# A transformer block in one kernel: new keys, engines and margins for the list schedule of its end

## The chip, the core and the metric

The kernel runs on one core of one Trainium2 chip. Its time is the device time of one execution in microseconds (us), start to end. The engines are named as in the profile: PE is the matrix engine (PEld its weight loads), DVE the vector engine, ACT the scalar engine, POOL is GpSimd, and SP is the engine that only issues DMAs here. Each of them works through its own queue of instructions in order, and waits at an instruction until the semaphores that it needs have been raised.

## The reference

One block of a transformer on 2048 rows of 512 values, all in float32: a LayerNorm with scale and shift from a condition vector, sliding-window attention (32 heads of 16, window 256), the output projection with a gate, a second LayerNorm, and a gated feed-forward network (FFN) with 1792 inner columns.

```python
    def _A_ref(x, wqkv, wo):
        ...
        scores = jnp.einsum("bhqd,bhkd->bhqk", q, k) * (Dh ** -0.5)
        ...
        mask = (idx[:, None] - idx[None, :] >= 0) & (idx[:, None] - idx[None, :] < W)
        scores = jnp.where(mask[None, None], scores, -1e9)
        p = _softmax(scores, axis=-1)
        o = jnp.einsum("bhqk,bhkd->bhqd", p, v)
        return (lambda x, *d: x.transpose(*d))(o, 0, 2, 1, 3).reshape(B, S, D) @ wo
    def _B_ref(x, w1, w3, w2):
        ...
        h = _silu(gate) * up
        out = jnp.einsum("bsf,fd->bsd", h, w2)
        return out
    ...
    h = _layernorm(x, axis=-1) * (1 + ca) + sa
    x = x + ga * _A_ref(h, A_wqkv, A_wo)
    h = _layernorm(x, axis=-1) * (1 + cb) + sb
    x = x + gb * _B_ref(h, B_w1, B_w3, B_w2)
```

## The kernel before

**Products.** Every precise product is made of three matmuls: an operand is split into a rounded high part (a copy on ACT) and the low rest (a subtraction on DVE or POOL), and high x high, high x low and low x high are summed in PSUM. So each new operand costs one ACT copy and one subtraction before PE can use it.

**Attention.** The rows are four blocks b of 512, the heads eight groups g of four. One unit is a pair (g, b); 32 units run in order u = 4g + b. A unit has a part a (products for queries and keys, L438), a part b (the row maxima: scores L485, maximum on DVE L494) and a part c (scores L753, masks by DVE L761 and L773 or by POOL L780 and L795, exponentials on ACT L768, values L721). At the end of a unit ACT copies its output (L815) and SP stores it to o_dr in DRAM (L818). The order of all that is written out by hand as offsets in time (the dictionary X).

**The end.** From the time TS = 229.9 in these offsets on, the remaining attention instructions are not simply emitted. They are put into a list with fixed times, which the function us() works out (KEY and the slopes TW), and everything else, the fillers, is given to a list scheduler, class Sched. A filler has an engine, an estimated duration, tiles that it reads and writes, and a key. The method deal() keeps the ready fillers of each engine in the order of their keys and takes, engine by engine, the first one that can start when the engine is free, or else the one that can start soonest; fixed operations go in when their time comes. A filler on PE that needs a result of ACT, DVE or POOL counts that result as ready PEM microseconds after its estimated end. A DMA (o.kb not zero) is given a time on one modelled wire (RATE KB per us), is kept out of the way of urgent row transfers of attention (QUIET), and its landing is the time at which its users become ready. The order that comes out is the order in which the instructions stand in the engines' queues; the chip knows nothing of the modelled times.

**The fillers.** The dictionary K holds most of their keys and some engines. In order of their work:

- load_x1 brings the residual rows x1 back (keys x1, xb, xl; tiles of the first half and of the second, x1a and x1b). load_wo loads and splits the output weights (key wo).
- o_sums (L1068 load, L1072 reciprocal on DVE, L1073 store) turns the softmax sums into factors (keys os and ol). o_part scales a quarter k of the outputs of block b: two loads (L1087, L1092), a product (L1104), a copy on ACT (L1096) and a subtraction (L1099). Keys pl (k = 3) and pe (the others); K["by"][b][k] names the engine of the product and that of the subtraction.
- o_proj multiplies block b by the output weights (L1116, 48 matmuls, key o[b] with steps of 0.27 for rows and 0.06 for quarters); add_stats adds the result to x1 on DVE and collects the sum for LayerNorm (L985, L990), and ACT squares it (L993).
- ln2 does the second LayerNorm of blocks 0 and 1 (key l2): the root on POOL (L1007), scaled rows on ACT (L1236), transposes on PE (L1250, keys l2 + 4 and l2 + 9), the modulation on ACT (L1254), sums and differences of the operands (L1267) and their splits (L1273, L1275).
- ffn does a step p of seven for one half of the rows. Each step has two sets (n = 0, 1) of seven up products, Strassen's scheme for two by two blocks (L1378), with sums on DVE and POOL (L1401 to L1421), a split (L1449, L1452), and the down products into x1 (L1471, L1476). Steps are fl apart, the first at f behind the modelled end of attention. load_w loads and splits the weights of a step (L1174, split L967 and L968, keys w0 and w), load_w2 those of the down product, and de puts off some of the last down products.
- Blocks 2 and 3 make the second half of the FFN. half_rows (key hr) and half_sums make their LayerNorm and operands during the first half and store them to DRAM, and load_b (key l3) loads the seven pairs of operands (L1353) and splits them at the start of the second half. K["be"] names the engines of the 14 subtractions (L968 into the tiles b).

PSUM has seven banks for all fillers, named st, mx and pj, beside the attention's po.

Of the kernel before, what the change touches and what calls it, by code (L numbers as in the profile page):

```python
# [112 lines left out]
class Sched:  # L113
# [36 lines left out]
    def deal(self):  # L150
# [5 lines left out]
        banks, fixed = list(self.banks), list(self.fixed)  # L156
        held = dict.fromkeys(CAPS, 0)
        given = dict.fromkeys(CAPS, 0)
        order, self.dealt = [], []

        def push(o):
            insort(ready[o.eng], (o.key, o.seq, o))

# [4 lines left out]
        while left:  # L168
            best = None
            for e, lst in ready.items():  # L170
                t, pick = free[e], None
                for key, seq, o in lst:
                    s = o.est
                    new = [b for b in o.bank if b.i is None]
                    if new:
# [6 lines left out]
                        s = max(s, at)  # L182
                    if o.kb:

                        b = max(s, t)
                        end = max(wire, b + 1.5) + o.kb / RATE + o.more - QUIET
                        s = max([s] + [u + 0.01 for u in self.urgent if b <= u < end])
# [24 lines left out]
            s, o = best  # L212
# [11 lines left out]
            if o.kb:  # L224
                s = max(s, lanes.pop(0))
# [17 lines left out]
                    banks[b.i] = b.end  # L243
                    held[b.use] -= 1
            for u in o.users:
                m = PEM if u.eng == "PE" and o.eng in ("ACT", "DVE", "POOL") else 0.0
                u.est = max(u.est, s + (o.lat + m if u.eng != o.eng or o.kb else o.occ))
                u.need -= 1
                if not u.need:
                    push(u)  # L250
# [5 lines left out]
INF = float("inf")  # L256
RATE = 320.0

QUIET = 1.5
KEY = 1.715  # L260
TS = 229.9

# [1 line left out]
def us(t):  # L264

    return KEY * (min(t, TW[0]) - TS + TW[2] * max(0.0, min(t, TW[1]) - TW[0]) + TW[3] * max(0.0, t - TW[1]))


TW = (231.0, 241.0, 0.8, 0.65)

KINDS = dict(product=("PE", 0.235), mix=("POOL", 1.25), qk_rows=("SP", 0.65), out=("ACT", 0.5), job=("POOL", 2.0),
             job_dma=("SP", 0.5), scores=("PE", 0.19), top=("DVE", 0.5), parts=("DVE", 0.4), turn=("PE", 0.11), cut=("ACT", 0.16),
# [1 line left out]
             far=("PE", 0.125), part=("POOL", 0.92), side=("ACT", 0.53), far_side=("ACT", 0.27), side_mask=("POOL", 0.92),  # L274
             side_probs=("ACT", 0.53), values=("PE", 0.66), cut_all=("ACT", 0.48), store=("SP", 0.45))
NPE = 3

PEM = 0.8

BY = ((("POOL", "POOL"),) * 3 + (("DVE", "DVE"),), (("POOL", "POOL"),) * 3 + (("DVE", "DVE"),),  # L280
      (("POOL", "DVE"),) * 3 + (("DVE", "DVE"),), (("POOL", "POOL"),) * 4)
K = dict(be=(('DVE', 'DVE'), ('DVE', 'POOL'), ('DVE', 'POOL'), ('POOL', 'POOL'), ('POOL', 'DVE'),
         ('POOL', 'DVE'), ('DVE', 'DVE')), hr=0.109, de=7.098, wo=-0.159, x1=5.764, xb=-29.382,
         xl=0.241, os=-0.129, ol=(-15.316, -4.484, -6.572, 4.956), pl=(3.999, 1.87, -4.828,
         102.62), pe=(0.982, -5.962, 56.258, 232.622), o=(1.381, 8.497, 20.124, -0.531), n=(1, 1,
         2, 1), w0=62.113, l2=0.424, f=1.543, fl=40.897, by=((('POOL', 'POOL'), ('DVE', 'DVE'),
         ('DVE', 'POOL'), ('DVE', 'DVE')), (('DVE', 'DVE'), ('DVE', 'POOL'), ('DVE', 'DVE'),
         ('DVE', 'POOL')), (('POOL', 'POOL'), ('POOL', 'DVE'), ('DVE', 'POOL'), ('POOL', 'DVE')),
         (('POOL', 'DVE'), ('DVE', 'POOL'), ('DVE', 'POOL'), ('DVE', 'POOL'))), w=0.559, dn=1.412,
         ds=0.003, l3=-0.027)  # L290
@with_exitstack
def block_kernel(ctx: ExitStack, tc: tile.TileContext, x, wqk, wv, wo, w13, w2, c, wmod, out):
    nc = tc.nc
# [653 lines left out]
    def dma(fn, key, reads, writes, kb=256, hold=False, occ=0.45, more=0.0):  # L947
        o = sch.op("SP", fn, occ, key, reads, writes, lat=2.0)
        o.kb, o.more = kb, more
        if hold:  # L950
            o.est = max(0.0, key)
# [7 lines left out]
    def on_eng(e):  # L959
        return nc.vector if e == "DVE" else nc.gpsimd  # L960

    def split(hi, lo, key, kh, kl, n=512, eng="POOL"):

        def src():
            return lo().bitcast(F32)
        kh, kl = (y if isinstance(y, list) else [y] for y in (kh, kl))
        sch.op("ACT", lambda: nc.scalar.activation(hi(), src(), AF.Copy), act(n), key, kl, kh)  # L967
        sch.op(eng, lambda: on_eng(eng).tensor_tensor(  # L968
            out=lo(), in0=src(), in1=hi().bitcast(F32), op=ALU.subtract),
               0.06 + 0.0024 * n if eng == "POOL" else 0.85, key, kl + kh, kl)  # L970
# [71 lines left out]
    def o_of(b):  # L1042
        return "p" if b == 1 else "o"
# [34 lines left out]
    def o_part(b, k, key):  # L1078
# [23 lines left out]
        dma(spread, key, [("r_dr", b, 2 * k), ("r_dr", b, 2 * k + 1)], [rn], 256, occ=0.67, more=0.1)  # L1102
        by, minus = K["by"][b][k]
        sch.op(by, lambda: on_eng(by).tensor_tensor(out=v["ot"], in0=v["ot"], in1=v["rt"], op=ALU.mult),  # L1104
# [4 lines left out]
    def o_proj(b, key):  # L1109
        for i in range(4):  # L1110
            bk = Bank("dn")
            t = 4 * b + i
            for k in range(KC):
                def go(i=i, k=k, bk=bk):
                    for n, (h, w) in enumerate(PARTS):
# [3 lines left out]
                sch.op("PE", go, 3 * MM[512], key + 0.27 * i + 0.06 * k,  # L1119
                       [y for kk in (range(K["n"][b]) if k == 0 else (k,)) for y in  # L1120
                        ((o_of(b), 0, kk), (o_of(b), 1, kk), ("wo", 0, kk), ("wo", 1, kk))], [bk])
# [222 lines left out]
    def load_b(key):  # L1344

        for n, m in enumerate((B11, T2, T3, T1, B21, T4, B22)):
            for k in range(2):
# [3 lines left out]
                else:  # L1351
# [3 lines left out]
                split(lambda m=m, k=k: BB[m, k][0], lambda m=m, k=k: BB[m, k][1], key + 0.1 * n,  # L1355
                      ("b", m, k, 0), ("b", m, k, 1), eng=K["be"][n][k])

    downs = []

    def ffn(half, p, key, fl):  # L1360
# [96 lines left out]
        def down():  # L1457
            load_w2(p, last, key + fl * (K["dn"] + K["ds"] * 8))
            for t in range(2):
                for i in range(4):  # L1460
                    at = 8 * half + 4 * t + i
                    bk = Bank("dn")
                    kk = key + fl * (1 + K["dn"] + K["ds"] * (4 * t + i)) + (
                        K["de"] if half and p == NP - 2 else 0.0)

# [140 lines left out]
```

## Time and profile before

| | |
|---|---|
| median of 3 runs | 959.67 us (958.03 to 962.35) |
| the profiled execution | 961.9 us |
| its span, first to last instruction | 960.2 us |
| mean granted clock of PE | 0.984 |
| HBM read, written | 85.72 MB, 34.61 MB |

The profile gives each instruction's start and duration, and for an idle spell of an engine the instruction or DMA that ended it (the releaser). A matmul's end is modelled, so a busy PE can still be a slow one: the granted clock (PEclk, 1.00 is full) has to be read beside it. A table by stretches has a row for each: the stretch in us from the span's start, its length, the busy time and count of PE, PEld, DVE, ACT and POOL, then PEclk, the share of the DMA engines that is busy, and GB/s. In a timeline a row has the start, the duration, the engine, the line, the operation and its tiles, and in square brackets the idle time before it with its releaser.

### The profile page before, as it was taken

What the parts mean: (1) busy time and instruction counts of PE and PEld (TensorE: products, weight loads), DVE (VectorE), ACT (ScalarE), POOL (GpSimd) and SP (SyncE); (2) the same over time, 40 slices, a digit from 0 to 9 for tenths busy, and PEclk for the clock granted to TensorE, in tenths of its full rate; (3) what the DMA queues carried; (4) which work ended last, traced back from release to release, by engine and by line L of the source; (5) the groups of instructions that cost most, each with busy time, mean ns of one, the idle gap of its engine ahead of it and who ended that gap; (6) DMA issues with size and microseconds to landing.
All of it is one profiled execution on the core that took longest, in us unless ns stands there. A gap on an engine that the chain in (4) does not pass through costs nothing.

```text
span 960.2 us, 16729 instructions
## 1 busy us (share of the span) xinstructions
PE 918.5 (96%) x5330; PEld 710.2 (74%) x5330; DVE 672.0 (70%) x1864; ACT 524.0 (55%) x1031; POOL 541.5 (56%) x691
## 2 busy tenths in 40 slices
PE   5999999999999999988986989999999999999998
PEld 2678677777777777755664878888888888888886
DVE  7576689898988989886568465765559645565455
ACT  3333677787867777766577653333446334433330
POOL 5211565666666576645565688977647456443420
PEclk9999999999999999999998999999999999999999
DMA  9531365555655655466870577754335413312102
GB/s 306 171 93 46 93 181 162 158 158 151 191 154 151 159 157 158 135 181 195 250 232 1 184 243 277 235 188 162 98 122 191 167 58 99 99 61 85 36 23 88
DMA packets 125020, 141.62 MB, mean 147 GB/s; under 512 B 60034, under 2 KB 72834, under 8 KB 124932
## 3 DMA queue, kind: packets, MB, share of 16 engines
q1 hardware_dynamic: 124212, 139.51, 47.7%
q10 hardware_dynamic: 720, 1.05, 0.4%
q8 instruction: 42, 0.69, 0.3%
q14 instruction: 46, 0.38, 0.1%
HBM read 85.72 MB, written 34.61 MB: 125 GB/s over the span
## 4 chain that ended last, share of the span: by engine, by line
PE 76%; DVE 8%; DMA 4%; POOL 3%; ACT 3%; issue 3%; SPq 2%; POOLq 0%; DVEq 0%; ACTq 0%
PE mx L1378 10%; PE st L1378 10%; PE pj L438 9%; PE st L753 8%; PE po L721 8%; PE mx L485 7%; PE mx L1471 7%; PE st L1471 6%; PE st L653 4%; PE pj L1378 3%; PE pj L1471 2%; POOL w L968 1%; POOL e L877 1%; PE mx L1116 1%; PE mx L572 1%
## 5 line engine op out<-in xcount | busy, mean ns | idle before, releaser
L494 DVE CUSTOM_DVE_ANT_0 junk<-mx,mskq 128x320 bf16<-128x320 f32 (+4 forms) x512 | 223.3, 464 | 36.1 <-PE mx L485 34.9
L968 POOL TENSOR_TENSOR w<-w,w 128x512 fp32r<-128x512 f32 (+2 forms) x56 | 107.4, 1931 | 117.1 <-ACT w L967 71.2
L485 PE MATMUL mx<-ringk,ringq 96*128 96x320 f32 (+4 forms) x512 | 154.5, 324 | 5.3 <-DVE mt L494 3.0
L753 PE MATMUL st<-ringq,ringk 98*128 98x256 f32 (+1 forms) x528 | 140.9, 335 | 7.1 <-DVE st L773 3.3
L780 POOL TENSOR_SCALAR_AFFINE_SELECT pt<-pt 128x256 f32<-128x256 f32 x224 | 91.4, 408 | 80.8 <-ACT pt L768 73.2
L438 PE MATMUL pj<-hT,wq 128*128 128x512 f32 x384 | 133.2, 405 | 1.6 <-DVE wq L427 0.8
L485 PEld LDWEIGHTS mx<-ringk,ringq 96*128 96x128 f32 x512 | 98.0, 192 | 45.3 <-DVE mt L494 24.7
L768 ACT ACTIVATE pt<-st 128x512 f32<-128x512 f32 (+1 forms) x198 | 115.4, 587 | 25.0 <-DVE st L773 9.3
L753 PEld LDWEIGHTS st<-ringq,ringk 98*128 98x128 f32 x528 | 90.9, 192 | 22.3 <-ACT pt L768 5.9
L721 PE MATMUL po<-pt,vS 128*17 128x384 f32 (+2 forms) x1408 | 93.1, 395 | 0.3 <-ACT pt L768 0.3
L438 PEld LDWEIGHTS pj<-hT,wq 128*128 128x128 f32 x384 | 68.5, 192 | 10.1 <-DVE wq L427 1.2
L1378 PE MATMUL mx<-b,w 128*128 128x512 f32 x270 | 67.7, 396 | 6.0 <-ACT t L1412 5.7
L1409 DVE TENSOR_TENSOR t<-mx,t 128x512 f32<-128x512 f32 x49 | 33.7, 688 | 45.6 <-PE mx L1378 26.0
L1378 PEld LDWEIGHTS mx<-b,w 128*128 128x128 f32 x270 | 51.2, 191 | 17.3 <-ACT t L1412 6.0
L1409 DVE TENSOR_TENSOR t<-st,t 128x512 f32<-128x512 f32 x47 | 32.4, 689 | 44.0 <-PE st L1378 22.8
L773 DVE COPY_PREDICATED st<-later,st 128x256 f32<-128x256 uint8 x112 | 47.4, 424 | 22.5 <-PE st L753 19.2
L721 PEld LDWEIGHTS po<-pt,vS 128*17 128x17 f32 x1408 | 34.8, 98 | 36.9 <-issue 19.0
L1449 ACT ACTIVATE wq<-g 128x512 fp32r<-128x512 f32 x28 | 17.7, 631 | 80.7 <-DVE g L1405 33.2
L761 DVE TENSOR_TENSOR st<-st,mskr 128x256 f32<-128x256 f32 x125 | 53.6, 429 | 8.8 <-PE st L753 8.8
L795 POOL TENSOR_SCALAR_AFFINE_SELECT sm<-sm 128x256 f32<-128x256 f32 x109 | 42.4, 406 | 28.3 <-ACT sm L785 27.2
L1378 PE MATMUL st<-b,w 128*128 128x512 f32 x234 | 57.9, 390 | 0.0
L451 POOL TENSOR_TENSOR qk<-qkr,qk 128x512 fp32r<-128x512 f32 x32 | 42.1, 1316 | 25.5 <-ACT qk L447 25.5
(262 smaller groups left out, 2009.5 us busy)
## 6 DMA issues: line engine op xcount, KB each, us to landing
ringk<-qk SPq DMA_DIRECT2D x96, 128.0 KB
ringq<-qk SPq DMA_DIRECT2D x192, 64.0 KB
o_dr<-os SPq DMA_DIRECT2D x32, 256.0 KB
w<-wsum SPq DMA_DIRECT2D x14, 512.0 KB
w<-w2g SPq DMA_DIRECT2D x14, 512.0 KB
jb<-in_w SPq DMA_DIRECT2D x24, 256.0 KB
wraw<-in_w SPq DMA_DIRECT2D x7, 768.0 KB
w<-wraw SPq DMA_DIRECT2D x14, 384.0 KB
```

The lines of the kernel that those rows point to most:

```text
L438: nc.tensor.matmul(v["ps"], WQ[g][w][:, n // 3], hTp(i, n // 3, b * BT, BT), start=(n == 0), stop=(n == 3 * KC - 1))
L485: nc.tensor.matmul(v[i][:, :n], both_queries(a, gs), keys(NS, a, (gs + 1) * HP - n, n), start=True, stop=True)
L494: nc.vector.tensor_tensor_reduce(out=junk[:, :n], in0=v[i][:, :n], in1=mskq[:, WK - n:], scale=1.0, scalar=-3e38, op0=ALU.add, op1=ALU.max ...
L721: nc.tensor.matmul(po[32 * i:32 * i + DH + 1, qb * P:(qb + nq) * P], vS[:, kb, 4 * g + i], pts[i // 2][:, i % 2, c0:c0 + nq], start=first, ...
L753: nc.tensor.matmul(o, keys(NM, a, kb * P, P), queries(a, q, n), start=q == lo, stop=not plus and q + n == hi, skip_group_check=True)
L761: nc.vector.tensor_tensor(out=ps, in0=ps, in1=mskk[:, p:p + 1].to_broadcast([P, 2, P]), op=ALU.add)
L768: nc.scalar.activation(held[u, j, a][:, :, :n], v[j, a, 0].rearrange("p (h q) k -> p h q k", h=2)[:, :, :n], AF.Exp, scale=SCALE)
L780: nc.gpsimd.affine_select(out=pt[:, :, 2 * m], in_=pt[:, :, 0], **w)
L968: sch.op(eng, lambda: on_eng(eng).tensor_tensor(out=lo(), in0=src(), in1=hi().bitcast(F32), op=ALU.subtract), 0.06 + 0.0024 * n if eng == ...
L1378: nc.tensor.matmul(ps(bk), WT[s, n][w][:, col], BB[t, k][r], start=start and c == 0, stop=stop and c == 5, skip_group_check=True)
L1409: return nc.vector.tensor_add(o, x, y)
L1471: nc.tensor.matmul(ps(bk), tiles[hk + (h,)][:, i * P:(i + 1) * P], w2_of(last, y, f), start=(m == 0), stop=(m == 5))
```

## The change

It touches only numbers and names that the list scheduler works with, and adds one term to it; no operation is added or taken away.

- PEM, the margin for PE after ACT, DVE and POOL, goes from 0.8 to 0.998.
- A new margin DM = 0.076 is added to the landing of a DMA for every user on an engine other than SP, for DMAs that start before the last fixed operation.
- QUIET goes from 1.5 to 1.487, and the last slope in TW from 0.65 to 0.583, so that the modelled times of the last attention units are shorter.
- K["by"]: block 1 swaps the subtraction engines of its quarters 2 and 3; in block 2 the product of quarter 1 moves from POOL to DVE; in block 3 the product of quarter 0 moves from POOL to DVE and its subtraction from DVE to POOL.
- K["be"]: of the 14 operand subtractions of the second half 4 instead of 8 are on DVE, and 10 instead of 6 on POOL.
- Most keys in K.

```diff
+        late = lambda o, u, s, stop=fixed[-1][0]: o.kb and u.eng != "SP" and s < stop
...
-                m = PEM if u.eng == "PE" and o.eng in ("ACT", "DVE", "POOL") else 0.0
+                m = PEM if u.eng == "PE" and o.eng in ("ACT", "DVE", "POOL") else DM if late(o, u, s) else 0.0
...
-QUIET = 1.5
+QUIET = 1.487
...
-TW = (231.0, 241.0, 0.8, 0.65)
+TW = (231.0, 241.0, 0.8, 0.583)
...
-PEM = 0.8
+PEM = 0.998
+DM = 0.076
...
-K = dict(be=(('DVE', 'DVE'), ('DVE', 'POOL'), ('DVE', 'POOL'), ('POOL', 'POOL'), ('POOL', 'DVE'),
-         ('POOL', 'DVE'), ('DVE', 'DVE')), hr=0.109, de=7.098, wo=-0.159, x1=5.764, xb=-29.382,
-         xl=0.241, os=-0.129, ol=(-15.316, -4.484, -6.572, 4.956), pl=(3.999, 1.87, -4.828,
-         102.62), pe=(0.982, -5.962, 56.258, 232.622), o=(1.381, 8.497, 20.124, -0.531), n=(1, 1,
-         2, 1), w0=62.113, l2=0.424, f=1.543, fl=40.897, by=((('POOL', 'POOL'), ('DVE', 'DVE'),
-         ('DVE', 'POOL'), ('DVE', 'DVE')), (('DVE', 'DVE'), ('DVE', 'POOL'), ('DVE', 'DVE'),
-         ('DVE', 'POOL')), (('POOL', 'POOL'), ('POOL', 'DVE'), ('DVE', 'POOL'), ('POOL', 'DVE')),
-         (('POOL', 'DVE'), ('DVE', 'POOL'), ('DVE', 'POOL'), ('DVE', 'POOL'))), w=0.559, dn=1.412,
-         ds=0.003, l3=-0.027)
+K = dict(be=(('POOL', 'DVE'), ('POOL', 'DVE'), ('DVE', 'POOL'), ('POOL', 'POOL'), ('POOL', 'POOL'),
+         ('POOL', 'POOL'), ('DVE', 'POOL')), hr=2.855, de=12.48, wo=-3.567, x1=16.6, xb=-38.041, xl=-26.167,
+         os=-0.13, ol=(-17.833, -5.162, -9.509, 10.002), pl=(11.205, -2.398, -4.869, 102.62), pe=(0.914, -2.635,
+         56.103, 231.635), o=(2.337, 8.384, 18.214, 9.324), n=(1, 1, 2, 1), w0=67.715, l2=2.802, f=2.068,
+         fl=40.1, by=((('POOL', 'POOL'), ('DVE', 'DVE'), ('DVE', 'POOL'), ('DVE', 'DVE')), (('DVE', 'DVE'),
+         ('DVE', 'POOL'), ('DVE', 'POOL'), ('DVE', 'DVE')), (('POOL', 'POOL'), ('DVE', 'DVE'), ('DVE', 'POOL'),
+         ('POOL', 'DVE')), (('DVE', 'POOL'), ('DVE', 'POOL'), ('DVE', 'POOL'), ('DVE', 'POOL'))), w=-2.134,
+         dn=1.412, ds=0.003, l3=-10.82)
```

## The prediction

> **What bounds the kernel now.** First the page: the span, the busy line, the strip of 40 slices and the chain that ended last.
>
> ```profile
> span 960.2 us, 16729 instructions
> PE 918.5 (96%) x5330; PEld 710.2 (74%) x5330; DVE 672.0 (70%) x1864; ACT 524.0 (55%) x1031; POOL 541.5 (56%) x691
> PE   5999999999999999988986989999999999999998
> PEclk9999999999999999999998999999999999999999
> PE 76%; DVE 8%; DMA 4%; POOL 3%; ACT 3%; issue 3%; SPq 2%; POOLq 0%; DVEq 0%; ACTq 0%
> ```
>
> TensorE bounds it, except in slices 18 to 24, which is just the part that the scheduler orders. The table of stretches (PE is the first busy time, PEclk third from the end) shows where PE is not full:
>
> ```profile
> 420.00:470.00 50.00, 42.66 (x301) 26.63 (x302) 30.86 (x92) 29.08 (x62) 23.58 (x36) 0.90 0.71 209
> 470.00:520.00 50.00, 38.81 (x171) 30.51 (x170) 37.20 (x58) 35.53 (x66) 33.75 (x23) 0.94 0.55 170
> 520.00:572.00 52.00, 51.90 (x235) 42.34 (x233) 27.92 (x45) 34.35 (x55) 36.03 (x32) 0.96 0.52 168
> 572.00:580.00 8.00, 5.66 (x20) 4.32 (x18) 5.78 (x7) 2.14 (x3) 6.18 (x7) 0.79 0.83 305
> 580.00:715.00 135.00, 135.00 (x597) 111.80 (x596) 81.86 (x109) 53.45 (x84) 100.83 (x91) 1.00 0.53 175
> 715.00:760.00 45.00, 44.83 (x197) 36.62 (x196) 34.22 (x43) 23.24 (x39) 32.60 (x18) 1.00 0.51 176
> 760.00:956.50 196.50, 196.50 (x867) 162.40 (x866) 110.82 (x162) 67.78 (x107) 75.72 (x44) 1.00 0.23 75
> 956.50:960.20 3.70, 0.01 (x1) 0.00 (x0) 0.69 (x1) 0.00 (x0) 0.00 (x0) 1.00 0.37 142
> ```
>
> PE idles 7.3 us in the last attention units, 11.2 in the output projection and second LayerNorm, 0.1, then 2.3: 21.0 us before 580. The lowered clock costs about (1 - PEclk) x busy: 4.3 + 2.3 + 2.1 + 1.2 = 9.9 us. After 580 only 0.2 us (at 715 to 760) and the last 3.7 us are without a matmul. The change removes no matmul, so it works on some 31 us and no more. PE's waits from 420 to 580 say what each stall ended with (total, times, longest):
>
> ```profile
> PE mx L1378 <- ACT t L1412: 5.7, 1, 5.7
> PE st L753 <- DVE st L773: 3.0, 2, 2.0
> PE st L1471 <- DVE x1a L1476: 2.3, 1, 2.3
> PE mx L1250 <- ACT wqr L1236: 2.2, 1, 2.2
> PE mx L485 <- DVE mt L494: 2.1, 2, 1.9
> PE mx L1116 <- DVE o L1099: 1.7, 1, 1.7
> PE mx L1250 <- ACT e L1236: 1.1, 3, 0.4
> ```
>
> **The change part by part. PE's margin (PEM 0.8 to 0.998) and the keys of projection and LayerNorm.** Queues are in order, so a matmul placed too early stops those behind it. Around the 2.2 us wait the timelines of PE and DVE show:
>
> ```profile
> 487.54 0.33 PE L1250 MATMUL mx<-ident,wqr 128*128 128x128 f32 x1 [2.23 <-ACT wqr L1236]
> 489.74 1.35 PE L1116 MATMUL pj<-wo,x1b 128*128 128x512 f32 x3
> 487.34 0.15 DVE L990 TENSOR_SCALAR nmB<-nmB 128x1 f32<-128x1 f32 x1
> 488.35 2.85 DVE L1104 TENSOR_TENSOR wq<-wq,wq 128x512 f32<-128x512 f32 x1
> 491.12 1.76 DVE L1099 TENSOR_TENSOR o<-wq,o 128x512 fp32r<-128x512 f32 x1
> 492.81 0.68 DVE L985 CUSTOM_DVE_ANT_0 x1a<-pj,x1a 128x512 f32<-128x512 f32 x1
> ```
>
> Four transposes (L1250) wait 2.2 + 1.1 = 3.3 us for ScalarE, and behind them stand the last three matmuls of block 1's projection (L1116 into pj). The sum that they feed (L985, 492.81) holds block 1's LayerNorm and so the FFN's start, and stands on DVE behind two operations of a later block (488.35, 491.12). With a longer margin the scheduler can put ready matmuls ahead of the transposes; block 3's projection, formerly foremost (key -0.531), now has 9.324, behind the first LayerNorm rows (2.802 + 4), and no longer goes before them. The best case moves the sum from 492.81 to the end of the small operation at 487.34 + 0.15: 5.3 us. The worst puts one more crowded vector operation ahead of it, 1.8 (the 1.76 row). I take **3.3 us gained**, the transposes' wait, since the margin acts on that wait directly. The 1.7 us wait on L1099 goes at nothing: removed, it only lengthens the 5.7 us wait behind it, for FFN's first tiles.
>
> That 5.7 us wait has a clock bill. Four rows of the table in 4 us stretches, for the two long stalls:
>
> ```profile
> 516.00:520.00 4.00, 0.97 (x2) 0.83 (x3) 3.97 (x4) 2.26 (x4) 3.38 (x3) 0.67 0.00 0
> 520.00:524.00 4.00, 4.00 (x11) 3.08 (x10) 3.32 (x6) 1.43 (x4) 1.25 (x1) 0.50 0.00 0
> 572.00:576.00 4.00, 1.66 (x8) 1.22 (x6) 3.70 (x4) 1.52 (x3) 2.34 (x3) 0.92 1.02 361
> 576.00:580.00 4.00, 4.00 (x13) 3.10 (x13) 2.08 (x3) 0.63 (x1) 3.84 (x5) 0.65 0.65 249
> ```
>
> After 5.7 us it is 0.33 x 0.97 + 0.50 x 4.00 = 2.3 us, after 2.3 us it is 0.08 x 1.66 + 0.35 x 4.00 = 1.5. If the first stall shrinks by 3.3 to 2.4, it pays about 1.5: **0.8 gained**, between 0 and 2.3. [...]
>
> **Late transfers (DM = 0.076) and the shorter model of the last attention units.** Vector and GpSimd waits for DMAs in 410 to 470:
>
> ```profile
> DVE wqr L1072 <- DMA wqr<-o_dr: 2.1, 2, 1.7
> DVE mT L1072 <- DMA qkr<-o_dr: 1.7, 1, 1.7
> DVE qkr L1104 <- DMA r_dr<-wqr: 1.3, 1, 1.3
> POOL qkr L1104 <- DMA qk<-r_dr: 3.7, 1, 3.7
> ```
>
> DVE stands 2.1 + 1.7 + 1.3 = 5.1 us, with attention's masks (L773) and maxima (L494) queued behind; those release PE in 5.1 us of its waits. DM is a twentieth of one such wait; over four waits it is 0.3. TW's last slope, 0.65 to 0.583, puts the last fixed operation (t = 260.3) 1.715 x 19.3 x 0.067 = 2.2 us earlier in the model, so attention goes ahead of more fillers. That can clear the last wait, 1.3. The first x1 tiles, held to 16.6 instead of 5.764, go at 0: nothing reads them before the projection sums. The keys of the scaling's parts (wo, os, ol, pl, pe) and QUIET's 0.013 us go at 0 as well: block 0's last part now stands behind block 1's (4.0 to 11.2), and attention's own matmuls hide that. Should either cover end, DVE stands for one load, at most POOL's 3.7. I take **1.6 gained**, between 5.1 and a loss of 3.7.
>
> **Other engines in the output scaling (by).** Block 2's second product goes from POOL to DVE; block 3's first product goes to DVE and its subtraction leaves it; block 1 swaps two subtractions. DVE gets one more product. Its price alone and its mean beside a busy POOL (485 to 520), and POOL's:
>
> ```profile
> L1104 DVE TENSOR_TENSOR qk<-qk,qk 128x512 f32<-128x512 f32 x1 | 0.7, 691 | 0.2 <-DMA qk<-o_dr 0.2
> L1104 DVE TENSOR_TENSOR wq<-wq,wq 128x512 f32<-128x512 f32 x2 | 3.5, 1772 | 0.2 <-DMA wq<-o_dr 0.2
> L1104 POOL TENSOR_TENSOR qkr<-qkr,qk 128x512 f32<-128x512 f32 x3 | 3.9, 1284 | 5.6 <-DMA qk<-r_dr 3.7 <-DMA qkr<-o_dr 1.9
> ```
>
> That is **0.7 lost** on the vector engine's path, since POOL loses the rival operation; 1.8 at worst, no loss if it fills an idle spell.
>
> **FFN steps (f, fl, w, hr).** Steps are keyed 40.1 us apart for 40.897, weights 2.7 us earlier, second-half rows 2.7 later. SP's weight DMAs move past h_dr stores and job stores; with PE full from 580 on, none of that counts except at 572, where the 2.3 us stall and its 1.5 us of clock stand. I take **1.0 gained**, a quarter of the 3.8, because nothing in the diff names that wait; the bounds are 3.8 gained and 2.3 lost (the same stall twice).
>
> **Second-half operands (be, l3).** Of 14 subtractions DVE keeps 4 of 8 and POOL has 10 for 6. The rows at that boundary:
>
> ```profile
> 724.87 8.64 POOL L968 TENSOR_TENSOR b<-b,b 128x512 fp32r<-128x512 f32 x5
> 744.75 1.73 DVE L968 TENSOR_TENSOR b<-b,b 128x512 fp32r<-128x512 f32 x1
> 746.54 0.50 PE L1378 MATMUL st<-b,wo 128*128 128x512 f32 x1 [0.17 <-DVE b L968]
> ```
>
> POOL takes 1.73 each here. The last operand releases PE with 0.17 us of waiting, so there is no slack; but that operand's subtraction no longer queues on DVE at 744.75, and w2 splits can follow it on POOL. Cost **0**, from 0.2 gained to 4 x 1.73 = 6.9 lost. Earlier load keys (l3) change little: a tile is loaded only after its last reader. [...]
>
> **The tail (de)** reorders down products that stand back to back; the last 3.7 us are one sum (0.69) and the stores: 0, at worst that sum again, 0.7.
>
> Sum: 3.3 + 0.8 + 1.6 - 0.7 + 1.0 = 6.0 us. The profiled execution took 961.9 us (span 960.2 and 1.7 around it), so 955.9; the median of the three runs is 959.67, 2.2 lower, which gives **953.7 us**.
>
> **The rivals.** (a) The wait only moves. DVE is busy 3.97 of 4 us in the 516 row and POOL 3.38, so LayerNorm's subtractions may bind whatever PE does: gains of 3.3 and 0.8 fall out, 1.6 + 1.0 - 0.7 = 1.9 remain, 957.8 us. Against it: the sum at 492.81 starts later than its matmuls would allow. (b) The keys keep their order, with DM and PEM too small to swap anything: 959.7. Against it: the engine swaps alone force another list. (c) Slower: the four subtractions added to POOL come last in its queue at the half boundary. It decides if the seventh pair of operands is ready after 746.4, when the 744.75 row ends now. Price: 6.9 us; with the other terms at nothing, 966.6. For it: no slack on PE there. Against it: 6.9 us more make POOL's 32.6 busy us of the 45 at most 39.5, and down products of the earlier step can fill PE.
>
> **How the numbers follow.** About 0.5%, 4.8 us, is what a measurement of this kernel tells from no change: faster is below 954.9, slower above 964.5. The forecast case gets 0.48, for a wait that the margin addresses by name; (a) 0.26; (b) 0.10; (c) 0.09, and 0.07 goes to losing ends of the other terms (a DVE wait of 3.7, the 572 stall twice). So faster 0.48, same 0.36, slower 0.16. All good ends together are 5.3 + 2.3 + 5.1 + 3.8 = 16.5, less 0.7 is 15.8, or 943.9: the low end, 944. The high end takes in (c): 967. The forecast's own range is 944 to 954.9.
>
> **What would show it.** Right: the transposes' wait (L1250) near 485 gone, L985's last x1a sum some 3 us earlier against the projection's end, FFN's first matmuls before 516, PE idle in 470 to 520 near 8 us. Attention's last units end 1 to 2 us earlier, with DVE's L1072 and L1104 waits below 4 us. No PE gap above 0.5 us at the half boundary. It would be wrong if PE's idle time before 580 stays at 20 us or more, if a new wait for a DMA stands on DVE, or if POOL's L968 rows end after PE's need.

## The result, and the profile after

| | before | after |
|---|---|---|
| median | 960.81 us (6 runs, 958.03 to 962.74) | 954.18 us (6 runs, 951.85 to 956.25) |
| ratio, 95% interval | | 0.9942 [0.9920, 0.9963] |
| again, in the last set of runs | 957.78 us (31 runs) | 953.88 us (12 runs), 0.9946 [0.9929, 0.9964] |
| the profiled execution | 961.9 us | 953.78 us |

So by the ratios the change gains 0.5 to 0.6%, 5.2 to 5.6 us of 960 (the bare medians differ by 6.6 us in the first set of runs and by 3.9 in the last); the forecast was 6.0 us, 953.7. From the page of the changed kernel, the span and the busy line:

```profile
span 952.1 us, 16722 instructions
PE 914.6 (96%) x5330; PEld 707.6 (74%) x5330; DVE 669.5 (70%) x1861; ACT 524.8 (55%) x1031; POOL 544.5 (57%) x694
```

PE is busy for 96% of the span, as before; where the time went shows only in the table of stretches (columns as in the table of before).

```profile
420.00:470.00 50.00, 44.66 (x311) 29.10 (x312) 31.80 (x90) 29.36 (x62) 24.48 (x36) 0.90 0.73 214
470.00:520.00 50.00, 41.50 (x178) 32.65 (x177) 37.26 (x59) 36.60 (x67) 32.62 (x21) 0.93 0.51 167
520.00:572.00 52.00, 49.50 (x229) 39.78 (x229) 31.71 (x45) 34.58 (x56) 39.28 (x35) 1.00 0.60 192
572.00:580.00 8.00, 8.00 (x37) 6.60 (x37) 7.09 (x10) 1.67 (x4) 7.61 (x10) 1.00 0.97 290
580.00:715.00 135.00, 134.70 (x595) 111.25 (x594) 78.99 (x107) 57.53 (x91) 100.14 (x88) 1.00 0.54 182
715.00:760.00 45.00, 45.00 (x200) 37.29 (x199) 33.44 (x44) 20.23 (x34) 31.94 (x20) 1.00 0.49 169
```

To read it as a ledger, call lost what PE idled plus (1 - PEclk) x its busy time. Before lost 11.6 us in 420 to 470, after 5.34 + 0.10 x 44.66 = 9.8. In 470 to 520 it is 13.5 against 8.50 + 0.07 x 41.50 = 11.4, in 520 to 580 5.7 against 2.5, and from 580 to 760 0.2 against 0.3. The gain in these two traces is thus 1.8 + 2.1 + 3.2 - 0.1 = 7.0 us, most of it around the start of the FFN and at 572, nothing at the half boundary. The ratios show less, 5.2 to 5.6; the traced execution of before (961.9) is 1.1 to 4.1 above the medians of its kernel (957.8 to 960.8).

PE's waits from 420 to 580 in the changed kernel (total, times, longest):

```profile
PE mx L1250 <- ACT wqr L1236: 3.0, 1, 3.0
PE mx L1116 <- ACT t L1254: 2.7, 1, 2.7
...
PE pj L1116 <- POOL o L1099: 1.5, 1, 1.5
PE st L1378 <- ACT t L1412: 1.3, 1, 1.3
```

The transposes' wait (L1250), which the forecast wanted gone, is longer here. The 2.3 us wait of L1471 is gone. The 5.7 us wait for FFN's tiles is down to 1.3, but two waits are new, 2.7 for ACT's L1254 and 1.5 for POOL's L1099, while the 1.7 for DVE's L1099 has gone. One trace shows these sizes only roughly: in two other executions of the same stretch (y_after and y_pem08, below) the first transpose waits 2.3 and 0.5 us, and the wait for FFN's tiles is 2.9 and 1.3. How the long wait was taken apart shows on PE's timeline, first before, then after:

```profile
511.20 1.29 PE L1378 MATMUL mx<-b,w 128*128 128x512 f32 x5
...
519.03 2.93 PE L1378 MATMUL mx<-b,w 128*128 128x512 f32 x6 [5.67 <-ACT t L1412]
521.76 3.36 PE L1116 MATMUL mx<-wo,o 128*128 128x512 f32 x9
```

```profile
508.33 2.51 PE L1116 MATMUL mx<-wo,o 128*128 128x512 f32 x6 [2.69 <-ACT t L1254]
510.64 1.48 PE L1116 MATMUL pj<-wo,o 128*128 128x512 f32 x3
...
514.17 1.52 PE L1378 MATMUL st<-b,w 128*128 128x512 f32 x6
516.98 1.66 PE L1378 MATMUL st<-b,w 128*128 128x512 f32 x6 [1.29 <-ACT t L1412]
```

Before starts its first FFN product at 511.20, and then stands for the second operand with more of the output projection (L1116) still to do behind it, at 521.76. After does more of that projection first and starts FFN 3 us later, at 514.17; the second operand is then nearly there. Counted over the trace from 430 on, 156 matmuls of L1116 go ahead of the second operand before and 168 after: twelve more, and a row of twelve such matmuls takes 2.88 us (at 479.51, shown further down). The operand itself is hardly earlier. To compare two executions, a common mark is needed: the matmul released at about 423 after a 2.0 us wait for a mask, which lies ahead of the first place where PE's programs differ (about 451).

```profile
424.23 0.39 PE L753 MATMUL st<-ringq,ringk 98*128 98x256 f32 x1 [2.03 <-DVE st L773]
468.31 0.41 PE L721 MATMUL po<-pt,vS 128*17 128x128 f32 x8 [0.29 <-ACT pt L768]
```

```profile
423.01 0.39 PE L753 MATMUL st<-ringq,ringk 98*128 98x256 f32 x1 [2.04 <-DVE st L773]
462.30 1.49 PE L721 MATMUL po<-pt,vS 128*17 128x384 f32 x24
```

These are that mark and the last attention matmuls (L721), before and after. Counted from the mark, the second operand releases PE after 519.03 - 424.23 = 94.8 us before and 516.98 - 423.01 = 94.0 after. Attention ends at 468.31 + 0.41 - 424.23 = 44.5 before and 462.30 + 1.49 - 423.01 = 40.8 after. The mark to the end of the span is 536.0 before and 529.1 after, 6.9 us, which agrees with the ledger's 7.0 of the same two traces.

How much of that is the change's, and how much the execution's? x_down, one of the experiments below, has the program of before on every engine up to about 571 us; its mark is at 421.09. Here are the first 46 us behind the mark and the next 94, first of before and then of x_down:

```profile
424.23:470.23 46.00, 41.26 (x294) 25.75 (x295) 28.63 (x85) 28.30 (x60) 23.72 (x36) 0.89 0.74 220
470.23:564.23 94.00, 82.71 (x368) 66.28 (x367) 61.89 (x98) 66.04 (x114) 62.34 (x43) 0.95 0.50 158
421.09:467.09 46.00, 42.18 (x304) 27.09 (x305) 30.24 (x88) 29.51 (x62) 23.82 (x36) 0.93 0.76 233
467.09:561.09 94.00, 83.62 (x370) 66.92 (x369) 61.99 (x96) 66.67 (x116) 64.83 (x46) 0.95 0.50 160
```

By the ledger before loses 9.3 + 15.4 us here and x_down 6.8 + 14.6, 3.4 us less with the same program. Its attention ends 42.1 us after the mark instead of 44.5, its second operand comes after 93.0 instead of 94.8, and PE's wait for it is 4.7 instead of 5.7. The changed kernel's trace loses 7.6 + 14.3 in the same two stretches, no less than x_down's. So a difference of 2 to 3 us between two traces, the 1.8 us of 420 to 470 for one, can't be put down to the change; what a change is worth is read from the ratios.

### The profile page after: what moved, and what is told of

The parts are those of the page before. It is cut to its first block, busy times and chain, and to the rows that moved or that the text cites. A ratio compares the mean times of both kernels' runs of the same rounds, so it can differ in the third digit from the quotient of the medians.

```text
span 952.1 us, 16722 instructions
## 1 busy us (share of the span) xinstructions
PE 914.6 (96%) x5330; PEld 707.6 (74%) x5330; DVE 669.5 (70%) x1861; ACT 524.8 (55%) x1031; POOL 544.5 (57%) x694
## 4 chain that ended last, share of the span: by engine, by line
PE 74%; DVE 8%; DMA 6%; POOL 3%; ACT 3%; issue 3%; SPq 2%; POOLq 0%; DVEq 0%; ACTq 0%
PE mx L1378 11%; PE st L1378 11%; PE pj L438 8%; PE st L753 7%; PE mx L1471 7%; PE st L1471 7%; PE mx L485 7%; PE po L721 7%; PE st L653 4%; PE pj L1378 3%; PE pj L1471 2%; DVE junk L494 1%; DMA w<-wraw 1%; PE mx L572 1%; DVE t L1267 1%
## 5 line engine op out<-in xcount | busy, mean ns | idle before, releaser
L968 POOL TENSOR_TENSOR w<-w,w 128x512 fp32r<-128x512 f32 (+2 forms) x56 | 106.4, 1914 | 112.0 <-ACT w L967 93.4
L721 PE MATMUL po<-pt,vS 128*17 128x384 f32 (+2 forms) x1408 | 92.5, 393 | 0.1
L1378 PE MATMUL st<-b,w 128*128 128x512 f32 x270 | 67.8, 391 | 1.3 <-ACT t L1412 1.3
L721 PEld LDWEIGHTS po<-pt,vS 128*17 128x17 f32 x1408 | 34.7, 98 | 36.4 <-issue 19.4
L1378 PE MATMUL mx<-b,w 128*128 128x512 f32 x240 | 59.9, 389 | 0.0
L1378 PEld LDWEIGHTS st<-b,w 128*128 128x128 f32 x270 | 50.5, 188 | 12.1 <-ACT t L1412 1.7
```

The source lines that it names most:

```text
L721: nc.tensor.matmul(po[32 * i:32 * i + DH + 1, qb * P:(qb + nq) * P], vS[:, kb, 4 * g + i], pts[i // 2][:, i % 2, c0:c0 + nq], start=first, ...
L968: sch.op(eng, lambda: on_eng(eng).tensor_tensor(out=lo(), in0=src(), in1=hi().bitcast(F32), op=ALU.subtract), 0.06 + 0.0024 * n if eng == ...
L1378: nc.tensor.matmul(ps(bk), WT[s, n][w][:, col], BB[t, k][r], start=start and c == 0, stop=stop and c == 5, skip_group_check=True)
```

## The experiments

Theory and rivals were sharpened as the runs came in. First theory: the margins make the gain, and what was forecast of the transposes and the sum L985 is how. Rivals: the engines or the keys do; or the sum's place binds nothing, because DVE and POOL bind that stage. Each ratio is against the kernel before in the same set of runs (its medians: 960.25, 958.32 and 957.78 us).

**Four parts alone.** m_margins: the kernel before with DM, QUIET and TW as changed, PEM and K as before. m_pem: PEM alone. m_engines: K["by"] and K["be"] alone. m_keys: all other keys alone.

```diff
# m_margins
-QUIET = 1.5
+QUIET = 1.487
-TW = (231.0, 241.0, 0.8, 0.65)
+TW = (231.0, 241.0, 0.8, 0.583)
+DM = 0.076
# m_pem
-PEM = 0.8
+PEM = 0.998
```

Expected of m_margins:

> The kernel before with DM, QUIET and TW of the change, and PEM, keys and engines as before. Theory A (the change's gain is a sum of small parts, as forecast): attention's last units gain 1.6 us, the rest stays: ratio 0.998, about 958. Theory B (the stalls only move, since a new list of the same work meets other waits): PE's idle time before 580 stays at 20 to 22 us and the time within 2 us of before. Either theory is hurt if the time moves by over 4 us.

Expected of m_pem:

> The kernel before with PEM = 0.998 alone. Theory A: the transposes' wait of 3.3 us (L1250) and a part of the clock's bill go: 3 to 4 us faster, ratio 0.996 to 0.997. Theory B: the transposes still wait, the sum L985 comes no earlier, and the time is within 2 us of before.

Expected of m_engines:

> The kernel before with the new engines in by and be alone. Theory A: 0 to 1 us slower (one more product on the vector engine, nothing at the half boundary): ratio 1.000 to 1.001. Rival C (POOL's queue decides at the half boundary): a PE gap of over 2 us between 735 and 760, and 4 to 7 us slower.

Expected of m_keys:

> The kernel before with the new keys alone (all of K but by and be). Theory A: 1 us faster, from the stall at 572. Theory D (the FFN's keys are the main part): that stall and its clock bill go whole, 3.5 to 4 us faster, ratio 0.996, with attention's end where it was.

Measured: m_margins 0.9958 [0.9943, 0.9972], m_pem 0.9965 [0.9944, 0.9986], m_engines 0.9999 [0.9984, 1.0015], m_keys 0.9995 [0.9979, 1.0012]. m_margins gains 4.0 us by its ratio, where theory A gave it 1.6 and theory B at most 2. The engines and the keys by themselves give nothing that these runs resolve, and theory D, the FFN's keys, is out: m_keys keeps the 2.3 us stall of L1471. The half boundary with ten subtractions on POOL, in m_engines:

```profile
715.00:760.00 45.00, 45.00 (x200) 37.24 (x200) 32.31 (x40) 23.17 (x38) 36.51 (x22) 1.00 0.49 167
```

POOL is busy 36.5 us there instead of 32.6, and PE does not idle at all: rival (c) of the prediction is out. m_pem comes out at theory A's number, but not by its way. On PE, up to about 538 us, its only difference from before is that the three matmuls of L1116 go ahead of the transposes; yet these still wait 1.3 + 1.1 us, the sum stands 493.17 - 426.13 = 67.0 us after the mark (67.2 in x_down, with the program of before), and the wait for FFN's second operand is the longest of all, 6.2 us. What its trace lacks is the stall of L1471.

**The slope alone, the two margins together, and two moves by hand.** x_tw takes the slope of m_margins only. x_margins_pem is m_margins with PEM as well. x_chain is the kernel before with the chain that the forecast spoke of moved by hand: the last products of block 1 go ahead of the four transposes, and L985 and L990 go on DVE directly behind them, ahead of three operations of blocks 2 and 3. x_down is the kernel before with DVE's L1405, which holds up L1471 at 572, put behind the first two sums L1476.

```diff
# x_tw
-TW = (231.0, 241.0, 0.8, 0.65)
+TW = (231.0, 241.0, 0.8, 0.583)
# x_chain, on the finished list
+    mm, add, mean = ops_of("PE", ("oproj", 1))[-1], *ops_of("DVE", ("oproj", 1))[-2:]
...
+    behind(mm, [add, mean] + sorted(late_, key=lambda o: order.index(o.fn)))
+    if order.index(turn.fn) < order.index(mm.fn):
+        behind(mm, [turn])
# x_down, on the finished list
+    behind(adds[1], [gate])
```

Expected of x_tw:

> The kernel before with the last slope of TW at 0.583 alone; DM, QUIET, PEM, keys and engines as before. If the slope carries what the three margins together gave (ratio 0.996, 955.8 us), this gives it too, 0.995 to 0.997. If the allowance for late transfers carries it, this is within 2 us of before.

Expected of x_margins_pem:

> The kernel before with PEM, DM, QUIET and TW of the change, and all of K (keys and engines) as before. If the keys and engines give nothing, this is as fast as the whole change, 0.994. If the gains of the slope and of PEM add, 0.992. If the keys carry a part that shows only together with the margins, this stays at 0.996 or above.

Expected of x_chain:

> The kernel before with one place changed by hand: on PE the last products of block 1's projection go ahead of the first four transposes, and on DVE their sum (L985, L990) goes ahead of three operations of later blocks. Theory A (the forecast's first term): LayerNorm and the FFN start 1.7 to 3.4 us earlier, and the time falls as much, ratio 0.9965 to 0.998. Rival (DVE and POOL bind the stretch, so the wait only moves): the FFN's second product, at 519.0 before, moves by less than 1 us and the time stays within 1.5 us.

Expected of x_down:

> The kernel before with one place changed by hand: on DVE one product of a gate (L1405, that waits for POOL until 571.0) goes behind the first two sums of the down product (L1476) instead of ahead of them. Theory A: the 2.3 us stall at 572 and its 1.5 us of clock go: 3 to 4 us faster, ratio 0.996. Rival (the stall only moves to the next operand): PE's idle time in 560 to 600 stays above 1.5 us and the time within 1.5 us of before.

Measured: x_tw 0.9962 [0.9947, 0.9976], x_margins_pem 0.9968 [0.9951, 0.9985], x_chain 0.9994 [0.9976, 1.0011], x_down 0.9986 [0.9968, 1.0004]. One number in TW by itself gives about two thirds of the whole gain, and PEM adds nothing to it that shows; had the two gains added, x_margins_pem would stand at 0.992, outside its interval. As it stays above 0.996, its own expectation reads it as a part that keys and engines give only together with the margins, but its interval overlaps that of the whole change. x_chain puts the sum where the forecast asked for it and gains nothing that shows. DVE's timeline there, and then PE's waits from 470 to 525:

```profile
482.27 0.68 DVE L985 CUSTOM_DVE_ANT_0 x1a<-pj,x1a 128x512 f32<-128x512 f32 x1
...
483.07 2.50 DVE L1104 TENSOR_TENSOR qk<-qk,qk 128x512 f32<-128x512 f32 x1
485.50 1.77 DVE L1104 TENSOR_TENSOR wq<-wq,wq 128x512 f32<-128x512 f32 x1
487.20 1.75 DVE L1099 TENSOR_TENSOR o<-wq,o 128x512 fp32r<-128x512 f32 x1
...
489.48 0.16 DVE L1004 TENSOR_SCALAR sqB<-sqB 128x4 f32<-128x4 f32 x1
```

```profile
PE mx L1378 <- ACT t L1412: 5.7, 1, 5.7
PE mx L1116 <- DVE o L1099: 3.4, 2, 1.7
...
PE mx L1250 <- ACT wqr L1236: 0.9, 1, 0.9
```

The mark is at 419.72 in this run. The sum stands at 482.27 - 419.72 = 62.6 against 492.81 - 424.23 = 68.6 before, 6.0 us earlier, and the transposes' wait has shrunk to 0.9. FFN's second operand releases PE at 513.29, 93.6 after the mark against 94.8: 1.2 us earlier, and 93.0 in x_down without any move, so not even that is shown. The three operations that stood ahead of the sum now stand behind it, as slow as ever (2.50, 1.77, 1.75), and their users wait for them: L1116 waits twice for L1099. And they still stand ahead of LayerNorm's next step on DVE, L1004, which also needs ACT's square of the sum (L993, only at 487.63): it comes 69.8 us after the mark, 71.3 before and 69.5 in x_down. The move brought the sum forward and left that step about where it was. The rival's numbers came out; that DVE and POOL bind the whole stage says too much. In before the stretch from the sum to the operand has two halves:

```profile
493.00:505.00 12.00, 12.00 (x68) 10.34 (x67) 6.14 (x18) 8.76 (x17) 3.70 (x4) 0.98 0.73 246
505.00:519.00 14.00, 6.20 (x24) 3.95 (x22) 13.82 (x13) 10.63 (x21) 10.59 (x7) 0.94 0.00 1
```

In the first PE is full and DVE half idle: the transposes of the last rows stand on PE behind a run of L1116 and start without a wait. In the second DVE is busy 13.82 of 14.00 us, with the sums and splits of FFN's operands (L1267, L1275).

x_down removes the 572 wait, as meant (8.00 us of 8.00 busy, at a clock of 1.00), but its interval takes in 1, and its point, 1.3 us (-0.4 to 3.1), is a third of the 3.8 that the prediction puts on that stall with its clock. So the stall was worth less than 3.8; whether it was worth the 2.3 us of idling these runs don't settle (the medians differ by 2.5).

**The changed kernel again, with one constant undone at a time, and with the hand move.** By then the theory was T: the slope carries the gain, by changing what fills FFN's first wait. y_after is the changed kernel unaltered, y_tw065 has the old slope in it, y_pem08 the old PEM, and y_chain has the move of x_chain in it.

```diff
# y_tw065
-TW = (231.0, 241.0, 0.8, 0.583)
+TW = (231.0, 241.0, 0.8, 0.65)
# y_pem08
-PEM = 0.998
+PEM = 0.8
```

Expected of y_after:

> The changed kernel once more, unaltered, beside the two that undo one constant each, so that all are read against the same runs of the kernel before. Theory T (the smaller last slope of the attention model carries the gain): 0.994 to 0.996 of the kernel before. Rival A (the constants' gains add: slope 0.996 and margin 0.9965 alone): 0.993. Rival R (half of the first measured gain of 0.6% came from the chip and the run, since three of the parts measured alone or together stopped at 0.996 to 0.997): 0.997.

Expected of y_tw065:

> The changed kernel with the last slope of the attention model back at 0.65, all else as changed. Theory T: the gain is mostly lost, 0.998 to 1.000 of the kernel before, with the last attention matmul back near 468 and a stall of 4 us or more before the FFN's second product. Rival A: half of it is lost, 0.9965. Rival P (what counts is any new list in which the stall at 572 falls away and the one at 516 is split; the slope is one of several ways to it): 0.995 to 0.997, with PE full from 572 to 580.

Expected of y_pem08:

> The changed kernel with PE's margin back at 0.8, all else as changed. Theory T: nearly nothing is lost, 0.995 to 0.996 of the kernel before. Rival A: half of it is lost, 0.9965 to 0.997. The prediction's first term (the margin removes the transposes' wait of 3.3 us): 3.3 us more than the changed kernel, 0.997 to 0.998, with the transposes' wait no smaller than the kernel before's 2.2 + 1.1 us.

Expected of y_chain:

> The changed kernel with, by hand, block 1's last sum and its mean put on the vector engine ahead of the three products of blocks 2 and 3 that stand before them. The prediction's first term (the sum's place on the vector engine holds LayerNorm and so the FFN's start): the sum comes 5 us earlier than 491.81, the FFN's first matmuls come some 3 us earlier, 0.991 of the kernel before. Rival (vector engine and GpSimd bind that stage whatever stands first, as the same move in the kernel before showed): the sum comes earlier, the FFN's second product by at most 1.5 us, and the time is within 0.2% of the changed kernel's.

Measured: y_after 0.9946 [0.9929, 0.9964], y_tw065 0.9972 [0.9954, 0.9991], y_pem08 0.9958 [0.9941, 0.9976], y_chain 0.9946 [0.9924, 0.9968]. Undoing the slope costs 955.93 - 953.88 = 2.05 us by the medians, about half of the gain, not nearly all as T had it; the intervals of the two overlap, so that even this half is not firm. The stall of 4 us or more that T expected there is 1.3. Undoing PEM costs 0.2 us by the medians, which is nothing, though rival A's 0.9965 lies inside its interval too. Indeed the program with the old PEM is the same as the changed kernel's on every engine up to about 590 us: with the new slope in, PEM moves no matmul of the transposes or of FFN's start at all. y_after leaves rival R (0.997) outside its interval; rival A (0.993) stays just inside. y_chain has its sum 482.44 - 420.49 = 62.0 after the mark, where the changed kernel has it at 491.81 - 423.01 = 68.8, and gains nothing by it that shows (952.76 against 953.88 us, the same ratio): the same answer as x_chain's, in the other list. Here too L1004 stays behind the moved operations (69.1 us after the mark, 70.8 in the changed kernel), and the transposes of the last rows start at 496.34 without a wait, behind 36 matmuls of L1116. No kernel measured has a lower ratio than the changed one.

**All of them side by side.** "Lost" is the ledger of 470 to 760, worked out from each trace as above; "to the end" is from the mark to the end of the span; "ahead" counts the matmuls of L1116 that go ahead of FFN's second operand; the two waits are PE's for that operand (L1412) and at L1471.

| kernel | ratio | lost, us | to the end, us | ahead | FFN wait | L1471 wait |
|---|---|---|---|---|---|---|
| before | 1 | 19.4 | 536.0 | 156 | 5.7 | 2.3 |
| m_engines | 0.9999 | 21.5 | 535.8 | - | 3.6 + 3.3 (for L1273, L1275) | none |
| m_keys | 0.9995 | 20.5 | 534.0 | 156 | 4.7 | 2.3 |
| x_chain | 0.9994 | 18.3 | 533.7 | 156 | 5.7 | 2.4 |
| x_down | 0.9986 | 15.2 | 530.3 | 156 | 4.7 | none |
| m_pem | 0.9965 | 18.7 | 532.0 | 156 | 6.2 | none |
| y_tw065 | 0.9972 | 13.2 | 531.4 | 168 | 1.3 | none |
| x_margins_pem | 0.9968 | 14.1 | 530.0 | 168 | 2.9 | none |
| x_tw | 0.9962 | 14.2 | 529.1 | 168 | 2.9 | none |
| m_margins | 0.9958 | 14.9 | 530.9 | 168 | 1.3 | none |
| y_pem08 | 0.9958 | 11.5 | 527.4 | 168 | 1.3 | none |
| after, y_after | 0.9942, 0.9946 | 14.2, 15.4 | 529.1, 529.6 | 168 | 1.3, 2.9 | none |
| y_chain | 0.9946 | 14.1 | 528.2 | 168 | 2.9 | none |

All lists with twelve more matmuls ahead of the operand and without the L1471 wait lose 11.5 to 15.4 us and stand at 0.9942 to 0.9972. Those with 156 stand at 0.9986 to 1 (m_engines, which stalls for other operands, at 0.9999), but for m_pem, whose one trace is of a run of 959.81 us, 3 us above its median; it is the one that this account doesn't explain. That suggests the filled wait as the mechanism, with the slope as one of the ways to it, as rival P of y_tw065 had it: x_tw gets there by the slope alone, y_tw065 without it, though its point, 0.9972, lies just outside P's numbers. T is thus at most half right.

The table does not prove it. The lost time of one trace does not rank the kernels: x_down loses 15.2 us and has its end 530.3 us after the mark, like the filled lists, and stands at 0.9986. And no run fills the wait and does nothing else: each list with 168 has lost the stall of L1471 as well. The nearest comparison is within one set of runs, x_tw (168, no such stall; median 953.91 us) against x_down (156, no such stall; 955.80): 1.9 us for the filler and all else in which the lists differ.

What is shown is that the slope alone is enough for about two thirds of the gain, that the gains of the slope and of PEM do not add, and that the sum's place, the half boundary, and the engines and the keys by themselves gain nothing that these runs can resolve. That the gain comes from the filled wait and the vanished stall at 572 is argued from the traces, and how it is shared between them, or between keys, engines, margins and slope, is open; the intervals are 0.3 to 0.4% wide.

## Why the prediction was right, and where its steps were wrong

The total was right (6.0 us forecast, 5.2 to 5.6 measured), and so, as far as the traces tell, was the place: PE's waits before 580, with nothing at the half boundary. The path to it was in large part wrong. The largest term did not come, and one that the sum does not have made up for it, so that the total came out this close is in good part luck.

- **3.3 us for the transposes' wait, "since the margin acts on that wait directly"**: wrong, and the largest term. The three matmuls did go ahead of the transposes, as the step said, but the wait did not go: the first transpose waits 3.0 us here, 2.3 in y_after and 0.5 in y_pem08 with the same program, against 2.2 and 2.1 (x_down) in the program of before, and the other three still wait for ACT behind it. The sum stood no earlier (68.8 us after the mark, 68.6 before). On PE's timeline after, the last projection products and the transposes:

```profile
479.51 2.88 PE L1116 MATMUL pj<-wo,x1b 128*128 128x512 f32 x12
...
486.02 0.33 PE L1250 MATMUL mx<-ident,wqr 128*128 128x128 f32 x1 [2.95 <-ACT wqr L1236]
```

  and on DVE's timeline after, what stands ahead of the sum:

```profile
485.85 1.57 DVE L1104 TENSOR_TENSOR qk<-qk,qk 128x512 f32<-128x512 f32 x1
487.34 1.75 DVE L1104 TENSOR_TENSOR qkr<-qkr,qk 128x512 f32<-128x512 f32 x1
489.02 2.86 DVE L1104 TENSOR_TENSOR wq<-wq,wq 128x512 f32<-128x512 f32 x1
491.81 0.68 DVE L985 CUSTOM_DVE_ANT_0 x1a<-pj,x1a 128x512 f32<-128x512 f32 x1
```

  PE is done with the sum's matmuls at 479.51 + 2.88 = 482.4, and DVE adds them 9.4 us later; before it was 492.81 - (489.74 + 1.35) = 1.7 us. The sign "L985 some 3 us earlier against the projection's end" turned round. x_chain and y_chain show no gain even from the move itself: LayerNorm's next step stays behind the same operations. The prediction had a part of the reason in rival (a), DVE busy 3.97 of 4 us, and gave it 0.26. That rival was right that the wait would not go and that DVE binds the last 14 us before the operand, and wrong about the sum, 957.8, because it saw nothing else to win in that stall.
- **What stood in its place.** The prediction treated FFN's 5.7 us wait as something that shrinks only if its chain gets shorter. It was filled instead: twelve more matmuls of the output projection, 2.88 us of work, go ahead of the operand, in the seven lists with 168. The term missing from the sum is that filler. What it is worth no run shows alone: the lost time in 470 to 520 falls from 13.5 to 11.4 us here and to 12.4 in y_after, and x_tw stands 1.9 us below x_down.
- **0.8 us for the clock**: not decided. In 470 to 572 the clock's bill falls from 2.3 + 2.1 = 4.4 to 0.07 x 41.50 = 2.9 in this trace, but it is 4.7 in y_after, the same program. The 1.2 at 572 is gone in both (clock 1.00 there).
- **1.6 us for the slope and DM**: attention did end earlier, by 3.7 us in these two traces; over all, it ends 40.3 to 41.8 us after the mark in the seven traces with the new slope and 42.0 to 44.5 in the seven with the old one. That is 2.4 us on average, a little above the sign's 1 to 2, and x_tw has it by the slope alone. The 1.8 us less lost in 420 to 470 is no proof of the term's size, since x_down shows as much with the program of before. DVE's waits for DMAs, which DM was to clear, are there as before: from 410 to 470 those of the changed kernel add up to 2.1 + 2.1 + 1.4 + 0.3 + 0.2 = 6.1 us, where before had 5.1, so the sign "below 4" failed. And the slope's larger effect may lie elsewhere, in the list behind attention, which the prediction did not ask for.
- **1.0 us for FFN's steps**, a quarter of 3.8: the whole stall at 572 went (5.66 busy of 8 before, 8.00 after), and x_down prices it at 1.3 us (-0.4 to 3.1), so the size is not contradicted. The reason given was wrong: it put this on FFN's keys, and m_keys, which has them, keeps the 2.3 us wait, while m_pem and x_tw, which haven't, lose it. Every new list deals DVE's L1405 and the sums L1476 anew, and nearly all of them happen to do better than the old one. What held PE before shows on DVE's timeline of the kernel before:

```profile
571.07 2.83 DVE L1405 TENSOR_TENSOR g<-t,g 128x512 f32<-128x512 f32 x1 [2.64 <-POOL t L1421]
573.83 1.27 DVE L1476 TENSOR_TENSOR x1a<-st,x1a 128x512 f32<-128x512 f32 x2
```

  DVE stands for POOL's L1421, then works 2.83 us at an operation, with the sums that PE waits for behind it.
- **0.7 us lost on the engines**: m_engines shows -1.5 to +1.4 us, so no loss was seen, and one of 0.7 is not excluded. The row of 0.7 that the prediction calls the price alone, at 487.74, has POOL's L968 beside it, and the worst price of 1.8 is below a row of the prediction's own, 2.85 at 488.35. **0 at the half boundary**: right; the 0.17 us wait is gone.
- **Block 3's key (-0.531 to 9.324), said to put its projection behind the LayerNorm rows**: wrong. With the old value put back into the changed kernel, the finished list is the same, so this edit does nothing.
- **The sign "FFN's first matmuls before 516"** told nothing: before had them at 511.20, after at 514.17. The sign that held was the idle time of 470 to 520, 8.5 us for "near 8".

## What to carry to other kernels

A stall on the busiest engine has two cures: shorten the chain that ends it, or put other work in front of it; ask for the second first, and look in the timeline for ready work that stands behind the stall. Before pricing an operation that "holds" a chain, ask what stands behind it on the same queues: here moving the sum 6 us forward left LayerNorm's next step behind the same operations on DVE, and FFN's operand came 1.2 us earlier at most. With a list scheduler, small edits of constants deal the whole list anew, so a gain belongs to the list, not to the constant; undo constants one at a time, and do not add up their gains. Trace one program twice before putting 2 us between two traces down to a change.

## What the runs showed of the hardware

**Executions of one program differ by more than the gain.** The mark at 423, up to which PE's program is the same in all these kernels, lies between 419.72 us (x_chain) and 426.13 (m_pem) in their traces: 6.4 us, more than the whole gain of 5.2 to 5.6. A common mark takes that out, but not all: from the mark on, before and x_down, the same program up to about 571 us, still differ by 2.4 us at the end of attention.

**The same gap, with and without a lowered clock.** y_after and the changed kernel are the same program. Here are the first one's rows for the stretch shown above from 508.33 on, and then the clock of 508 to 512, y_after first and the changed kernel second:

```profile
509.49 1.66 PE L1116 MATMUL mx<-wo,o 128*128 128x512 f32 x6 [2.71 <-ACT t L1254]
510.99 0.85 PE L1116 MATMUL pj<-wo,o 128*128 128x512 f32 x3
...
518.14 2.82 PE L1378 MATMUL st<-b,w 128*128 128x512 f32 x6 [2.90 <-ACT t L1412]
```

```profile
508.00:512.00 4.00, 2.51 (x11) 2.04 (x12) 3.81 (x8) 3.86 (x7) 2.31 (x2) 1.00 0.00 0
```

```profile
508.00:512.00 4.00, 3.67 (x10) 2.84 (x11) 3.82 (x6) 4.00 (x8) 2.33 (x3) 0.61 0.00 0
```

After 2.71 us of idling three matmuls take 0.85 us, after 2.69 us they take 1.48. The slow one then waits 1.29 us for FFN's operand, the fast one 2.90, and pays with a lowered clock behind that wait instead (0.57 in 518 to 522, and 2.82 us for six matmuls against 1.66). From the first of these rows to the operand it is 8.65 us in both (516.98 - 508.33 and 518.14 - 509.49): the lowered clock in front of the wait cost nothing, it only used up the wait. It also corrects the prediction's clock argument, by which a stall of 2.4 us pays about 1.5: a gap of about that size is not sure to cost. Behind 2.69 us of idling the clock stood at 0.61, behind 2.71 us of the same wait at 1.00.

**Beside POOL's work a DVE operation took four times its time.** The product L1104 took 0.69 us alone (at 492.60 in the changed kernel, where POOL idles from 491.33 to 494.06) and 2.86 beside POOL at 489.02 there; the product L1405 took 2.83 at 571.07 in the kernel before, where POOL's L968 runs from 571.00 for 2.36 us. POOL's row beside the 2.86:

```profile
483.85 7.48 POOL L968 TENSOR_TENSOR w<-w,w 128x512 fp32r<-128x512 f32 x4
```

Four subtractions take 7.48 us, 1.87 each. DVE's 2.86 is 0.69 + 2.17, where the prediction took 1.8 in all as the worst price of a crowded operation; and the one at 487.74 in the kernel before takes 0.69 although POOL works beside it. That POOL's work is what slows DVE is read from the overlap; no run takes that work away.
